# Windowed attention and a rational feed-forward: unpadded float32 scores in row halves, and an order of issue left to the scheduler

## The chip, the core and the metric

The kernel runs on one core of a Trainium2 chip. The metric is device microseconds from start to end of one execution; a run's time is set beside the median of several. The engines are named as the profile names them: PE (TensorE, matrix products and transposes), PEld (its weight loads), DVE (VectorE), ACT (ScalarE), POOL (GpSimd) and SP (SyncE, which here only issues transfers). Each engine takes its instructions in one order, fixed when the program is built.

## The reference

Two parts in a row: attention with a window and a few global keys, and a feed-forward network whose activation is a ratio of polynomials.

```python
scores = q @ k.T / 8 - 2.0 ** -(h + 1) * dist        # per head h; B, H, S, D = 4, 8, 768, 64
keep = (key < n_global) | ((0 <= rel) & (rel < n_local))   # n_global = 8, n_local = 96
a = softmax(where(keep, scores, -1e9))
x = concat_heads(a @ v)                              # 3072 tokens x 512
h = x @ w_in                                         # 512 x 2048
g = (a0 + a1*h + a2*h**2 + a3*h**3) / (1 + |b0|*|h| + |b1|*h**2 + 1e-6)
out = g @ w_out                                      # 2048 x 512
```

All inputs are float32 but for the weights' and coefficients' stored form, which the kernel decodes. With a window of 96 a block of 128 queries needs its own block of keys and the one before it; the eight global keys are copied over columns of the older block that are no longer needed.

## The kernel before

The work is cut into 96 attention units: a unit is one block of 128 tokens and one pair of heads (2 x 64 columns), four units to a block, eight to a chunk of 256 tokens. `unit(u)` gives the chunk, the block, the pair p, the batch and the block's number i in its batch. Units 0 to 23 (`PLAIN = 24`), which are the first batch, work in plain float32; the later ones work in a split of two parts, and are not changed. Each unit goes through steps: `st_load` (q and k of two units in one transfer each), `st_qkT` (transposes of q and k on PE), `st_qkE` (they are scaled out of PSUM), `st_score` (products on PE, then masks and row minimum in one DVE operation for each head, `tensor_tensor_reduce`), `st_soft` (exponential on ACT), `st_sums`, `st_norm` (POOL), `st_pT` (transposes of the probabilities), `st_pv` (product with v) and `st_x`. The feed-forward of a chunk runs in steps `st_ffn1`, `st_ew1` to `st_ew4` and `st_ffn2` some ten units behind; in the first chunk its products are plain float32 too. Weights come as 32 transfers of 512 KB that SP issues (`fetch`), and are decoded on ACT, POOL and DVE (`decode`) and later split (`split_w`).

In the early units a head's keys fill 64 of the 128 rows of the array, as two heads share a transposed tile. The kernel multiplies all 128 rows: `qz` holds for each head a copy of q in which the other head's 64 rows are zero (cleared once at the start, three buffers in turn), and `kF` the keys of the current and the previous block:

```python
nc.scalar.activation(out=qz[ds_, x, :], in_=tk[ds_, 0, :], func=AF.Copy, scale=float(2.0 ** (2 * p + x - 2)))
nc.scalar.copy(out=pl.kF[:, p, i % 2, :], in_=tk[:, 1, :])
nc.tensor.matmul(out=blocks_of(s_ps[:, x], i), lhsT=qT[:, x, :], rhs=blocks_of(pl.kF[:, p], i), ...)
```

Transposes, scores and products with v take turns in three PSUM banks (`ps_t`, `bufs=3`); a score tile `s` holds both heads of a unit in one bank. The product with v of two heads writes to different halves of the array's columns (`o_ps[x * D:(x + 1) * D]`).

Order: the loop over t gives each step a priority (`PRI_A` in the first part, `PRI` behind), and a scheduler that estimates times lists each engine's instructions by it. On top of that `ORDER` is a written list for PE, DVE, ACT, POOL and SP that fixes the order of the first steps, up to about unit 36 and the feed-forward step 25, some 320 us; `pin()` chains the instructions in that order and puts all others behind. Behind it the scheduler's order holds.

Of the kernel before, what the change touches and what calls it, by code (L numbers as in the profile page):

```python
# [9 lines left out]
F32 = mybir.dt.float32  # L10
FR = mybir.dt.float32r
# [35 lines left out]


ORDER = dict(
    PE=(  # L50
# [25 lines left out]
    ),  # L76
    DVE=(
# [132 lines left out]
def tile_kernel(ctx: ExitStack, tc: tile.TileContext, q, k, v, n_global, n_local,  # L210
# [258 lines left out]
    sp = {}  # L469
    tqk = {}  # L470
    qTs = {}
    prob = {}
    pTs = {}
    ops = {}

# [500 lines left out]
```

## Time and profile before

| | |
|---|---|
| median of 3 runs | 748.33 us (747.7 to 750.04) |
| profiled execution: span from first to last instruction | 747.0 us |
| PE busy | 723.6 us (97%) |
| DVE, ACT, POOL busy | 605.0, 576.5, 457.2 us |
| granted clock of PE, mean | 0.996 |

The profiled execution's own time is its span; the runs' times include what lies around it. Busy time is an average over parts of the kernel with different limits, so the rows below are taken by stretch. An idle time in brackets or behind an arrow names what ended it. Matmuls are pipelined, and their ends are modelled: the time from one start to the next is a better price of a matmul in a run than its duration.

### The profile page before, as it was taken

To read this page: it belongs to the slowest core of one execution; us is meant where nothing else is said; L and a number is where in the kernel's file an instruction comes from. 1 tells how busy PE (TensorE), PEld (TensorE's weight loads), DVE (VectorE), ACT (ScalarE), POOL (GpSimd) and SP (SyncE) were. 2 spreads that over 40 slices of the span, in tenths; PEclk is the share of its full clock that TensorE was granted. 3 is DMA by queue.
4 is the path that set the end of the run, shared out by engine and by line. 5 is a ranking of instruction groups with operands and counts; after the bars stand their busy time and mean duration, and the time that the engine had idled before them with its cause. 6 is when DMAs were issued, how large, how long until landed. Compare 5 with 4: busy or idle time off the path is not lost.

```text
span 747.0 us, 15315 instructions
## 1 busy us (share of the span) xinstructions
PE 723.6 (97%) x5026; PEld 629.0 (84%) x5026; DVE 605.0 (81%) x1437; ACT 576.5 (77%) x1303; POOL 457.2 (61%) x504
## 2 busy tenths in 40 slices
PE   5799899999999999999999999999999999999996
PEld 4576566888988989999999999998998989998995
DVE  5888978888889797878888888887888888875565
ACT  6889776887987886877887878877877878866664
POOL 3366997776576675655665657656666566664441
PEclk9999999999999999999999999999999999999999
DMA  8986310124535443334334334334434333210000
GB/s 252 300 271 195 99 30 15 50 58 103 140 106 139 141 115 90 115 108 109 110 96 119 114 104 123 115 101 99 125 92 125 117 87 98 84 48 2 29 1 33
DMA packets 123581, 79.49 MB, mean 106 GB/s; under 512 B 82532, under 2 KB 104036, under 8 KB 123492
## 3 DMA queue, kind: packets, MB, share of 16 engines
q1 hardware_dynamic: 122288, 77.89, 36.4%
q8 instruction: 42, 0.69, 0.4%
q10 hardware_dynamic: 1204, 0.52, 0.3%
q14 instruction: 47, 0.39, 0.2%
HBM read 35.92 MB, written 6.29 MB: 57 GB/s over the span
## 4 chain that ended last, share of the span: by engine, by line
PE 86%; DVE 4%; DMA 4%; ACT 3%; issue 2%; POOL 1%; SPq 0%; DVEq 0%; ACTq 0%; POOLq 0%
PE h L374 34%; PE acc L450 32%; PE o L623 5%; PE s L541 5%; PE tp L597 3%; DMA r<-in_moe_w_in_dram 2%; PE acc L445 2%; PE s L536 2%; PE tk L486 1%; PE h L366 1%; DMA vt<-in_v_dram 1%; ACT pr L565 1%; DMA nat<-in_q_dram 1%; DVE w_3f L310 0%; DVE pr L555 0%
## 5 line engine op out<-in xcount | busy, mean ns | idle before, releaser
L581 POOL TENSOR_SCALAR pr<-pr,stats 128x256 f32<-128x256 f32 (+1 forms) x176 | 157.6, 906 | 75.5 <-DVE stats L572 46.7
L374 PE MATMUL h<-xh,win_l 128*128 128x256 f32 x704 | 198.2, 282 | 0.0
L407 POOL TENSOR_TENSOR fa<-fa,fs 128x512 f32<-128x512 f32 x95 | 123.7, 1302 | 100.4 <-ACT fs L400 88.8
L450 PE MATMUL acc<-wout_l,g 128*128 128x512 f32 x352 | 139.3, 396 | 0.0
L374 PEld LDWEIGHTS h<-xh,win_l 128*128 128x128 f32 x704 | 133.1, 189 | 2.3 <-issue 1.4
L430 POOL TENSOR_TENSOR g<-fu,g 128x512 fp32r<-128x512 f32 x87 | 113.9, 1309 | 34.4 <-ACT g L429 23.1
L398 ACT ACTIVATE fu<-h,coef 128x512 f32<-128x512 f32 (+1 forms) x97 | 74.9, 772 | 41.0 <-PE h L374 37.5
L565 ACT ACTIVATE pr<-pr,stats 128x256 f32<-128x256 f32 (+1 forms) x192 | 92.9, 487 | 16.9 <-DVE stats L555 16.4
L419 DVE SCALAR_TENSOR_TENSOR fu<-fu,coef,q 128x512 f32<-128x512 f32 (+1 forms) x97 | 71.6, 738 | 24.7 <-ACT q L415 23.3
L414 ACT ACTIVATE fs<-fa,coef 128x512 f32<-128x512 f32 (+1 forms) x97 | 69.6, 717 | 27.1 <-POOL fa L407 25.5
L405 DVE TENSOR_TENSOR fu<-fu,h 128x512 f32<-128x512 f32 (+1 forms) x97 | 65.8, 678 | 29.8 <-ACT fs L400 27.4
L450 PEld LDWEIGHTS acc<-wout_l,g 128*128 128x128 f32 x352 | 66.2, 188 | 11.9
L518 ACT ACTIVATE kq<-tk 64x256 fp32r<-64x256 f32 x144 | 54.3, 377 | 26.9 <-DVE kq L519 15.8
L406 DVE SCALAR_TENSOR_TENSOR fu<-fu,coef,h 128x512 f32<-128x512 f32 (+1 forms) x97 | 71.7, 739 | 2.0
L420 DVE SCALAR_TENSOR_TENSOR q<-fa,coef,q 128x512 f32<-128x512 f32 (+1 forms) x97 | 72.2, 744 | 0.0
L600 DVE COPY pT<-tp 128x512 f32<-128x512 f32 (+1 forms) x75 | 48.4, 646 | 25.1 <-PE tp L597 24.4
L400 ACT ACTIVATE fs<-h,coef 128x512 f32<-128x512 f32 (+1 forms) x97 | 66.2, 682 | 2.6 <-DVE fu L421 1.1
L519 DVE SCALAR_TENSOR_TENSOR kq<-tk,kq 64x256 fp32r<-64x256 f32 x144 | 60.8, 422 | 8.6 <-ACT kq L518 4.2
L421 DVE SCALAR_TENSOR_TENSOR fu<-q,fu 128x512 f32<-128x512 f32 (+1 forms) x97 | 66.1, 682 | 1.6
L399 ACT ACTIVATE fa<-h,coef 128x512 f32<-128x512 f32 (+1 forms) x97 | 65.5, 676 | 0.3 <-DMA out_dram<-o 0.3
L429 ACT CAST g<-fu 128x512 fp32r<-128x512 f32 (+1 forms) x89 | 54.9, 617 | 8.4 <-DVE fu L421 7.5
L415 ACT ACTIVATE q<-fs 128x512 f32<-128x512 f32 (+1 forms) x97 | 57.2, 590 | 0.9
(258 smaller groups left out, 2008.4 us busy)
## 6 DMA issues: line engine op xcount, KB each, us to landing
pm<-pr SPq DMA_DIRECT2D x60, 256.0 KB
mv<-nat SPq DMA_DIRECT2D x36, 256.0 KB
qT<-kq SPq DMA_DIRECT2D x144, 64.0 KB
r<-in_moe_w_in_dram SPq DMA_DIRECT2D x16, 512.0 KB
r<-in_moe_w_out_dram SPq DMA_DIRECT2D x16, 512.0 KB
nat<-in_q_dram SPq DMA_DIRECT2D x48, 128.0 KB
vt<-in_v_dram SPq DMA_DIRECT2D x48, 128.0 KB
nat<-in_k_dram SPq DMA_DIRECT2D x46, 128.0 KB
```

Source lines behind the costliest of these rows:

```text
L374: nc.tensor.matmul(out=hps[f][:, y, :], lhsT=w[:, fs], rhs=x[:, ct, :], start=(n == 0), stop=(n == 3 * NCT - 1))
L398: nc.scalar.activation(out=u, in_=h, func=AF.Identity, scale=a3, bias=a2)
L400: nc.scalar.activation(out=s, in_=h, func=AF.Square, scale=b1)
L406: nc.vector.scalar_tensor_tensor(out=u, in0=u, scalar=a1, in1=h, op0=ALU.add, op1=ALU.mult)
L407: side(f).tensor_tensor(out=a, in0=a, in1=s, op=ALU.add)
L414: nc.scalar.activation(out=s, in_=a, func=AF.Ln, bias=q1)
L419: nc.vector.scalar_tensor_tensor(out=u, in0=u, scalar=a0, in1=r, op0=ALU.add, op1=ALU.mult)
L420: nc.vector.scalar_tensor_tensor(out=r, in0=a, scalar=q1, in1=r, op0=ALU.add, op1=ALU.mult)
L430: side(f).tensor_tensor(out=g[:, 1, ys], in0=u, in1=g[:, 0, ys], op=ALU.subtract)
L450: nc.tensor.matmul(out=acc, lhsT=gs[f][:, z, y, ts], rhs=w, start=(ft == 0 and n == 0), stop=(ft == NFT - 1 and n == 2))
L565: nc.scalar.activation(out=d, in_=d, func=AF.Exp, scale=-1.0, bias=st[:, x:x + 1], accum_out=st[:, 2 + 2 * x:3 + 2 * x])
L581: nc.gpsimd.tensor_scalar(out=d, in0=d, scalar1=st[:, 6 + x:7 + x], scalar2=None, op0=ALU.mult)
```

## The change

For units 0 to 23 the padded `qz` falls away. `kF` gets a third slot for q, and one scaling takes q and k of a unit out of PSUM together, both by 2^(p-1). `st_qkT` transposes two units into one bank, at even t. The new `st_pair` issues the scores of two units: for each unit both heads in turn, head x with rows x*64 to x*64+63 and a bank of its own, chained so that this order holds. The reductions then use a mask at half size for the second head, as in the later units; the half masks are made at the start and not at unit 24. The copy of the global columns (`kGF`) is made on POOL out of `kF`, and copied back for two units at once. `st_pT` of two units is issued at even t. `ORDER`, `pin` and `traced` are removed, so the scheduler orders everything.

```diff
-ORDER = dict(
-    PE=("qkT0 score0:1 qkT1 score0:1 score1 qkT2:1 pT0:1 qkT2:1 pT0:1 score2 qkT3 pT1 pv0:6 score3:1 ..."),
...
     def st_qkT(u):
+        kind, unit_r = (FR, ident_r) if u >= PLAIN else (F32, ident)
+        tk = pl.ps_t.tile([P, 2, 2, P], kind, tag="t", name=f"tk{u}")
+        for y in range(2):
+            for z in range(2):
+                n = nat[u // 2][:, 1 - z, 2 * y:2 * y + 2, :]
+                nc.tensor.transpose(out=tk[:, y, z, :], in_=n.rearrange("p a d -> p (a d)"), identity=unit_r)
+            tqk[u + y] = tk[:, y]
...
         if u < PLAIN:
-            qz = pl.qz[:, u % 3]
-            for x in range(2):
-                ds_ = slice(x * D, (x + 1) * D)
-                nc.scalar.activation(out=qz[ds_, x, :], in_=tk[ds_, 0, :], func=AF.Copy,
-                                     scale=float(2.0 ** (2 * p + x - 2)))
-            nc.scalar.copy(out=pl.kF[:, p, i % 2, :], in_=tk[:, 1, :])
+            nc.scalar.activation(out=pl.kF[:, p, i % 2:3:2 - i % 2, :], in_=tk, func=AF.Copy, scale=half)
             if i == 0:
-                nc.scalar.copy(out=pl.kGF[:, p, :], in_=tk[:, 1, 0:G])
-            qTs[u] = qz
+                nc.gpsimd.tensor_copy(out=pl.kGF[:, p, :], in_=pl.kF[:, p, 0, 0:G])
             return
...
+    def st_pair(u):
+        c, t, p, b, i = unit(u)
+        banks = [pl.ps_t.tile([P, 2, 2, P], F32, tag="t", name=f"s{u + x}") for x in range(2)]
+        began = len(nc.cur_bb.bb.instructions)
+        for y in range(2):
+            for x in range(2):
+                own = pl.kF[x * D:(x + 1) * D, p + y]
+                nc.tensor.matmul(out=blocks_of(banks[x][:, y], i), lhsT=own[:, 2, :], rhs=blocks_of(own[:, 0:2, :], i),
+                                 start=True, stop=True)
+            sps[u + y] = [banks[x][:, y] for x in range(2)]
+        run = list(nc.cur_bb.bb.instructions)[began:]
+        for x, y in zip(run, run[1:]):
+            behind_of(y, x, "row halves in turn")
+        if 1 <= i < NT - 1:
+            nc.gpsimd.tensor_copy(out=pl.kF[:, p:p + 2, i % 2, 0:G], in_=pl.kGF[:, p:p + 2, :])
...
-            m0, m = (mask0, masks) if u < PLAIN or x == 0 else (pl.half0, pl.halves)
+            m0, m = (half0, halves) if x else (mask0, masks)
...
-                scale=-(2.0 ** -(h + 1 if u < PLAIN else 2 * p + 1)), scalar=3e38, op0=ALU.add, op1=ALU.min, accum_out=st[:, x:x + 1])
+                scale=-(2.0 ** -(2 * p + 1)), scalar=3e38, op0=ALU.add, op1=ALU.min, accum_out=st[:, x:x + 1])
...
-        pl.kF = pl.early.tile([P, NPAIR, 2, P], F32, name="kF")
+        pl.kF = pl.early.tile([P, NPAIR, 3, P], F32, name="kF")
...
-        for x in range(2):
-            nc.gpsimd.memset(pl.qz[(1 - x) * D:(2 - x) * D, :, x, :], 0.0)
...
+        for m, full_m in ((half0, mask0), (halves, masks)):
+            nc.vector.tensor_scalar(out=m, in0=full_m, scalar1=0.5, scalar2=None, op0=ALU.mult)
...
+            if t % 2 and t < PLAIN:
+                on("score", st_pair, t - 1)
...
-            if t - 2 < PLAIN:
+            if t % 2 == 0 and t - 2 < PLAIN:
                 on("pT", st_pT, t - 2)
+                on("pT", st_pT, t - 1)
...
-        pin()
```

## Rows read from the trace of the kernel before

**Rows 1.** Busy microseconds (and instructions) of each engine by stretch, granted clock, DMA.
```profile
core 0: us, PE busy (x) PEld busy (x) DVE busy (x) ACT busy (x) POOL busy (x), PEclk, DMA share, GB/s
0.00:36.00 36.00, 23.73 (x128) 16.23 (x128) 25.34 (x100) 25.22 (x87) 11.39 (x33) 0.95 0.92 276
36.00:80.00 44.00, 41.71 (x220) 30.37 (x221) 38.41 (x90) 37.41 (x92) 30.49 (x38) 1.00 0.72 230
80.00:115.00 35.00, 33.53 (x156) 22.16 (x154) 30.18 (x58) 25.78 (x59) 32.04 (x30) 1.00 0.15 38
115.00:165.00 50.00, 49.84 (x316) 39.95 (x317) 42.71 (x94) 40.08 (x94) 36.19 (x33) 1.00 0.14 36
165.00:320.00 155.00, 154.41 (x1156) 139.79 (x1156) 132.50 (x330) 124.15 (x285) 101.91 (x113) 1.00 0.43 120
320.00:680.00 360.00, 360.00 (x2672) 327.42 (x2671) 297.71 (x710) 283.24 (x622) 220.82 (x240) 1.00 0.36 102
680.00:747.00 67.00, 60.36 (x386) 53.06 (x385) 38.16 (x61) 40.64 (x70) 24.32 (x19) 0.98 0.05 18
```
**Rows 2.** The chain that ended last, 0 to 62 us: start, length, what.
```profile
5.63 7.70 DMA r<-in_moe_w_in_dram
...
22.91 0.18 ACT qz L505
...
31.87 0.04 ACT kF L507
```
**Rows 3.** The same chain, 62 to 125 us.
```profile
70.72 2.84 DVE w_3f L310 x2
...
113.09 1.68 DVE w_14f L310
```
**Rows 4.** Busy time by stretch, of the early units' score line (L536) alone.
```profile
0.00:36.00 36.00, 10.61 (x32) 6.90 (x32) 0.95 0.92 276
36.00:115.00 79.00, 10.76 (x40) 6.95 (x40) 1.00 0.47 145
115.00:165.00 50.00, 6.73 (x24) 4.21 (x24) 1.00 0.14 36
```
**Rows 5.** PE in order of time, 150 to 166 us: start, length, line, operation.
```profile
155.15 1.02 PE L536 MATMUL s<-kF,qz 128*128 128x256 f32 x4
156.01 0.38 PE L492 MATMUL tk<-ident,nat 128*128 128x128 f32 x2
```
**Rows 6.** PE in order of time, 60 to 80 us.
```profile
66.52 0.66 PE L623 MATMUL o<-pT,vt 128*64 128x128 f32 x8
67.11 1.13 PE L536 MATMUL s<-kF,qz 128*128 128x256 f32 x4
```
**Rows 7.** PE in order of time, 286 to 296 us.
```profile
288.94 1.97 PE L623 MATMUL o<-pT,vt 128*64 128x128 f32 x32
290.84 0.50 PE L450 MATMUL acc<-w_10h,g 128*128 128x512 f32 x1
```
**Rows 8.** Groups of ACT's instructions by line and shape, 0 to 180 us.
```profile
line engine op names shapes xcount | busy us, mean ns | idle before us <-releasers
L505 ACT ACTIVATE qz<-tk 64x128 f32<-64x128 f32 x48 | 12.9, 268 | 7.8 <-PE tk L492 7.5
...
L507 ACT COPY kF<-tk 128x128 f32<-128x128 f32 x24 | 6.4, 265 | 0.3
...
L600 ACT COPY pT<-tp 128x256 f32<-128x256 f32 x4 | 1.5, 372 | 0.0
```
**Rows 9.** The same view of DVE, 0 to 180 us.
```profile
L555 DVE CUSTOM_DVE_ANT_0 pr<-s,masks 128x256 f32<-128x256 f32 x40 | 15.4, 418 | 2.4 <-PE s L536 1.5 <-PE tp L597 0.7
```
**Rows 10.** Who waited for whom, 0 to 130 us: total us, times, longest.
```profile
ACT w_13f L305 <- DMA r<-in_moe_w_out_dram: 2.8, 1, 2.8
...
PE s L536 <- DVE stats L555: 1.6, 1, 1.6
```
**Rows 11.** The waits of SP's own queue, 0 to 130 us.
```profile
SPq L627 <- PE o L623: 25.8, 5, 14.8
SPq L244 <- PE tk L492: 19.9, 4, 11.4
```

More of the change, by code (lines that the diff above doesn't have):

```diff
@@ L46 @@
 LO_V = (13, 15, 17, 19, 21, 23, 25, 27, 29, 31)
-ORDER = dict(
-    PE=(
[25 rows of a table removed]
-    ),
-    DVE=(
[25 rows of a table removed]
-    ),
-    Activation=(
[19 rows of a table removed]
-    ),
-    Pool=(
[11 rows of a table removed]
-    ),
-    SP=(
[9 rows of a table removed]
-    ),
-)
 PRI = dict(load=0, score=50, soft=100, sums=120, ffn1a=150, qkT=200, pv=250, qkE=300, x=350, split=400, ew3=450, norm=500,
@@ L468, in tile_kernel @@
     masks = const.tile([P, 3, P], BF16, name="masks")
+    half0 = const.tile([P, P], BF16, name="half0")
+    halves = const.tile([P, 3, P], BF16, name="halves")
     sp = {}
@@ L471, in tile_kernel @@
     qTs = {}
+    sps = {}
     prob = {}
@@ L479, in st_qkT @@
     def st_qkT(u):
-        p = unit(u)[2]
-        if u >= PLAIN:
-            tk = pl.ps_t.tile([P, 2, 2, P], FR, tag="t", name=f"tk{u}")
-            for y in range(2):
-                for z in range(2):
-                    n = nat[u // 2][:, 1 - z, 2 * y:2 * y + 2, :]
-                    nc.tensor.transpose(out=tk[:, y, z, :], in_=n.rearrange("p a d -> p (a d)"), identity=ident_r)
-                tqk[u + y] = tk[:, y]
-            return
-        tk = pl.ps_t.tile([P, 2, P], F32, tag="t", name=f"tk{u}")
-        for z in range(2):
-            n = nat[u // 2][:, z, 2 * (p % 2):2 * (p % 2) + 2, :]
-            nc.tensor.transpose(out=tk[:, z, :], in_=n.rearrange("p a d -> p (a d)"), identity=ident)
-        tqk[u] = tk
+        kind, unit_r = (FR, ident_r) if u >= PLAIN else (F32, ident)
[5 more added lines that the diff above has]
+            tqk[u + y] = tk[:, y]
     def st_qkE(u):
@@ L513, in st_qkE @@
         raw = tk.bitcast(F32)
-        half = float(2.0 ** (p - 1))
         for x in range(2):
@@ L527, in st_qkE, with behind_of @@
         qTs[u] = qT
+    def behind_of(x, prev, why):
+        tc.add_manual_dep(x, prev.name, mybir.DependencyInfo(mybir.DependencyClass.NoSync,
+                                                             mybir.DependencyReason.DATA), reason=why)
+    def st_pair(u):
[13 more added lines that the diff above has]
+            nc.gpsimd.tensor_copy(out=pl.kF[:, p:p + 2, i % 2, 0:G], in_=pl.kGF[:, p:p + 2, :])
@@ L529, in st_score @@
     def st_score(u):
         c, t, p, b, i = unit(u)
-        qT = qTs.pop(u)
-        s_ps = pl.ps_t.tile([P, 2, 2, P], F32, tag="t", name=f"s{u}")
-        for x in range(2):
-            h = 2 * p + x
-            if u < PLAIN:
-                nc.tensor.matmul(out=blocks_of(s_ps[:, x], i), lhsT=qT[:, x, :], rhs=blocks_of(pl.kF[:, p], i),
-                                 start=True, stop=True)
-                continue
-            rhs = pl.kq[:, h, 0:2, :] if i else pl.kq[:, h, 0:1, :].broadcast_to([P, 2, P])
-            for z, lhsT in enumerate((pl.kq[:, h, 2, :], qT[:, x, :])):
-                nc.tensor.matmul(out=s_ps[:, x], lhsT=lhsT, rhs=rhs, start=(z == 0), stop=(z == 1))
@@ L542, in st_score @@
-        if 1 <= i < NT - 1 and u < PLAIN:
-            nc.gpsimd.tensor_copy(out=pl.kF[:, p, i % 2, 0:G], in_=pl.kGF[:, p, :])
-        elif 1 <= i < NT - 1:
+        if u < PLAIN:
+            s_ps = sps.pop(u)
+        else:
+            qT = qTs.pop(u)
+            s_ps = pl.ps_t.tile([P, 2, 2, P], F32, tag="t", name=f"s{u}")
+            for x in range(2):
+                h = 2 * p + x
+                rhs = pl.kq[:, h, 0:2, :] if i else pl.kq[:, h, 0:1, :].broadcast_to([P, 2, P])
+                for z, lhsT in enumerate((pl.kq[:, h, 2, :], qT[:, x, :])):
+                    nc.tensor.matmul(out=s_ps[:, x], lhsT=lhsT, rhs=rhs, start=(z == 0), stop=(z == 1))
+            s_ps = [s_ps[:, x] for x in range(2)]
@@ L545, in st_score @@
+        if 1 <= i < NT - 1 and u >= PLAIN:
             hs = slice(2 * p, 2 * p + 2)
@@ L555, in st_score @@
             nc.vector.tensor_tensor_reduce(
-                out=blocks_of(pr[:, x], i), in0=blocks_of(s_ps[:, x], i), in1=mask(x),
-                scale=-(2.0 ** -(h + 1 if u < PLAIN else 2 * p + 1)), scalar=3e38, op0=ALU.add, op1=ALU.min, accum_out=st[:, x:x + 1])
+                out=blocks_of(pr[:, x], i), in0=blocks_of(s_ps[x], i), in1=mask(x),
+                scale=-(2.0 ** -(2 * p + 1)), scalar=3e38, op0=ALU.add, op1=ALU.min, accum_out=st[:, x:x + 1])
         prob[u] = (pr, st)
@@ L662, in windowed @@
         pl.early = scope.enter_context(tc.tile_pool(name="early", bufs=1))
-        pl.kF = pl.early.tile([P, NPAIR, 2, P], F32, name="kF")
+        pl.kF = pl.early.tile([P, NPAIR, 3, P], F32, name="kF")
         pl.kGF = pl.early.tile([P, NPAIR, G], F32, name="kGF")
-        pl.qz = pl.early.tile([P, 3, 2, P], F32, name="qz")
         nc.scalar.dma_start(out=ni[:, 0:2], in_=n_local.bitcast(I32).partition_broadcast(1))
@@ L675, in windowed @@
         make_identity(nc, ident)
-        for x in range(2):
-            nc.gpsimd.memset(pl.qz[(1 - x) * D:(2 - x) * D, :, x, :], 0.0)
         nc.vector.tensor_copy(out=ident_r, in_=ident)
@@ L689, in windowed @@
         window_masks(nc, scr, mask0, masks, nl, ng)
+        for m, full_m in ((half0, mask0), (halves, masks)):
+            nc.vector.tensor_scalar(out=m, in0=full_m, scalar1=0.5, scalar2=None, op0=ALU.mult)
         load_coef()
         base = tc.cur_priority
-        here = nc.cur_bb.bb
-        made, began = {}, len(here.instructions)
-        def traced(token, fn, *args):
-            n = len(here.instructions)
-            fn(*args)
-            for x in list(here.instructions)[n:]:
-                made.setdefault((token, x.engine), []).append(x)
-        def behind_of(x, prev, why):
-            tc.add_manual_dep(x, prev.name, mybir.DependencyInfo(mybir.DependencyClass.NoSync,
-                                                                 mybir.DependencyReason.DATA), reason=why)
-        def halve_masks():
-            for m, full_m in ((pl.halves, masks), (pl.half0, mask0)):
-                nc.vector.tensor_scalar(out=m, in0=full_m, scalar1=0.5, scalar2=None, op0=ALU.mult)
-        def pin():
-            for name, words in ORDER.items():
-                eng = getattr(mybir.EngineType, name)
-                chain, taken = [], {}
-                for word in words.split():
-                    token, _, count = word.partition(":")
-                    own = made[token, eng]
-                    a = taken.get(token, 0)
-                    b = taken[token] = a + int(count) if count else len(own)
-                    chain += own[a:b]
-                for x, y in zip(chain, chain[1:]):
-                    behind_of(y, x, "order of the first steps")
-                known = {x.name for x in chain}
-                for x in list(here.instructions)[began:]:
-                    if x.engine == eng and x.name not in known and "Boundary" not in type(x).__name__:
-                        behind_of(x, chain[-1], "behind the first steps")
         def turn(f):
@@ L750, in behind @@
             def behind(n):
-                now, past = t - n, t - n - 1
-                return [u for u in ((past,) if past >= PLAIN else ()) + ((now,) if now < PLAIN else ())]
+                past = t - n - 1
+                return [past] if past >= PLAIN else [t - 1, t] if t % 2 and t < PLAIN else []
             if t % 2 == 0:
@@ L768, in windowed @@
                 pl.kG = pl.late.tile([P, H, G], FR, name="kG")
-                pl.halves = pl.late.tile([P, 3, P], BF16, name="halves")
-                pl.half0 = pl.late.tile([P, P], BF16, name="half0")
-                tc.cur_priority = base + 1000 * t
-                traced("halves", halve_masks)
                 on("split", st_move, t)
             ffn("ffn1a", st_ffn1, f, 0)
-            if t < PLAIN or t % 2 == 0:
+            if t % 2 == 0:
                 on("qkT", st_qkT, t)
@@ L811, in windowed @@
                 for key in pieces(kind, j):
-                    traced("dec" + "".join(map(str, key)), decode, key)
+                    decode(key)
             if step:
```

9 lines of the change are left out of this document (4 added, 5 removed), and 89 rows, old and new, of tables (Activation, DVE, PE, Pool).

## Prediction

> **What bounds the kernel now.** I read the busy time by stages first, since an average over 747 us hides that the kernel has three parts [rows 1]. From 165 to 680 us TensorE (PE) is busy 154.4 of 155 and 360.0 of 360 us at full granted clock: nothing but PE work counts there. From 0 to 36 us it idles 12.3 us of 36, and the 16 DMA engines are busy 92% of the time. From 36 to 115 us PE idles only 3.8 us, but VectorE (DVE) is busy 68.6 of 79 us and GpSimd (POOL) 32.0 of 35 us in the second half: several engines are close to full. From 115 us on PE is full. All the idle time of PE is 747.0 - 723.6 = 23.4 us: 12.3 before 36 us, 3.8 up to 115, 0.8 up to 320, and 6.6 behind 680 us. The change touches only units 0 to 23, whose scores are done by 165 us, so it can save PE work and can move the first two of these idle sums; the last part it only shifts.
>
> Then the chain that ended last, to see which stage lets a saving through. Up to 62 us it runs over weight transfers (one piece of 7.7 us) with short stretches of ScalarE (ACT) between, nine of them copies of q and k, from 22.91 to 31.87 us, 2.0 us together [rows 2]. Up to 115 us it goes over the decoding of weights on DVE, 2.84 us for two operations at 70.7 us, 1.68 at 113 [rows 3]. Only behind that is it PE nearly without a break. So a microsecond of PE work is worth a microsecond after 115 us, something between nothing and that from 36 to 115, and nothing before 36.
>
> **The change part by part.** *Scores in row halves.* A float32 product is two PE instructions. Four of them, both heads of a unit, take 0.86 us from start to next start (155.15 to 156.01) [rows 5]: 0.215 us for 256 columns, and by columns 0.108 for 128. Two units in a run are 8 x 0.215 = 1.72 us today. With 64 rows for each head the two heads sit in different halves of the array's rows; if they run side by side, the second head's first instruction starts with the first head's second, and eight instructions take five places: 5 x 0.215 = 1.08. No row of before shows row halves. The nearest are the two heads of the product with v, which sit in different halves of the columns, in the same order: eight instructions of 128 columns take 0.59 us to the next start [rows 6], against 8 x 0.108 = 0.86 one by one and 0.54 for five places; 32 take 1.90 us [rows 7], against 3.44 and, for 17 places, 1.83. So such halves do run side by side, at a price of 0.05 to 0.07 us a run. I take 1.72 - 1.08 - 0.05, about 0.6 us, saved for a pair of units. The score instructions lie 32 before 36 us, 40 from 36 to 115 and 24 behind [rows 4], four to a unit: 8, 10 and 6 units, so 4, 5 and 3 pairs. Behind 115 us the 3 pairs save 1.8 us in full; the 5 pairs before it up to 3.0, of which I take half, 1.5, because DVE and POOL are nearly as full as PE there; those before 36 us nothing. Together -3.3; ends -1.8 and -4.8, and 0 if the halves don't overlap.
>
> The Trainium skill (TensorEngine Tiling (Array Packing), Key Properties) speaks against this: changing the tiling mode drains TensorE, and this change goes into the row mode and out of it twelve times. The trace agrees only in that a run with column halves costs 0.05 to 0.07 us over its places [rows 6, 7]; by the rule alone, with a price left open, the sum would lie somewhere above mine. Its other condition (Gotcha 1), that row halves don't share a PSUM bank, the new code meets: each head has a bank of its own.
>
> *One copy of q and k.* Today a unit costs ACT two scalings of 64x128 and a copy of 128x128: 2 x 0.268 + 0.265 = 0.80 us [rows 8]. The new form is one scaling of 128x256; the nearest row of that size out of PSUM takes 0.372 [rows 8]. That is 0.43 us a unit and 10 us of ACT over 24 units, but ACT limits only where the chain crosses it: 2.0 us in the nine pieces [rows 2], of which the same share, 54%, is 1.1. Weight transfers stand next in line there, so I take -0.5; ends 0 and -1.1. The copy of the eight global columns of four units goes from ACT to POOL and each copy back into the keys serves two units; the two clears of the padding fall away; the two halvings of the masks go to the start. POOL is busy 11.4 us of the first 36 and DVE 25.3 [rows 1], so I cost these at nothing; without that cover they would be fractions of a microsecond.
>
> *Two units at a time.* Of the three banks that transposes, scores and products with v share, one pair now holds two until four reductions over them have run. One takes 0.418 us [rows 9], so 1.7 us at the least, and more when a decode of 1 to 2 us stands between [rows 3]. Behind a score that waits for a bank stand, in PE's order, the feed-forward matmuls. Before, one such wait of 1.6 us is in the trace for 24 units [rows 10]. One in each of the 8 pairs behind 36 us would be 12.8, none 0. A pair holds twice as much half as often, so I stay near the one row and add +0.4. The even unit's scores wait for the odd one's copy, about 0.4 us, hidden in the transfers of the fill and later behind feed-forward work. Both transposes of a load now run together, so its buffer comes free one unit earlier; SP waited 19.9 us for such transposes in the first 130 us [rows 11]. The loads would start sooner, in a stage where DMA is 92% busy [rows 1], so they compete with the weights: 0.
>
> *The order of issue.* The written order of PE, DVE, ACT, POOL and SP falls away for roughly the first 320 us. What it is worth, the trace shows only by its neighbour: from 320 to 680 us, where the scheduler already orders, PE idles 0.0 us of 360 [rows 1]. Wherever PE has a backlog, another order costs nothing. Before 115 us it can cost: engines take their queues in order, and an instruction placed too early stops all behind it, as ACT did for 2.8 us on a late weight [rows 10], and SP for 14.8 us behind a single wait at the line that rereads the global rows of v [rows 11]; behind such a wait on SP stand the fetches of weights, for which decode, then feed-forward, wait. At best all idle time of PE from 36 to 115 us goes, -3.8; at worst one more hold of SP reaches PE, +14.8. The order before already contains waits of both kinds and still leaves PE 3.8 us of idle time, so another list is likelier to add than to remove. I take +0.6, about a third of one wait of the 1.6 us kind.
>
> **The sum.** -3.3 - 0.5 + 0.4 + 0.6 = -2.8 us. The profiled execution spans 747.0 us and the median of the runs is 748.3, so 1.3 us lie around the span or between runs. The span would be 744.2, the median 745.5. For this kernel 0.3% is 2.2 us, about the least that can be told from no change: same means 746.1 to 750.6.
>
> **The rivals.** *The new order costs more than the scores save (slower).* Place: the fill and the decoding, before 115 us. Mechanism: SP or ACT held by a wait placed too early, so that weights come later and the feed-forward starts later. For it: the waits of rows 10 and 11, and a stage in which DMA, DVE and POOL are all nearly full. Against it: PE's backlog from 115 us. It decides from 5 us of new idle time on (2.8 + 2.2); one hold of 5 to 15 us gives 748 + 2 to 748 + 12, so 751 to 760. Chance 0.31.
>
> *The saving is hidden.* What bounds 36 to 115 us is decoding on DVE and POOL, so only the 1.8 us behind 115 us stay, and a wait for a bank or a slightly worse order takes them: 746 to 750. For it: the chain over DVE up to 115 us [rows 3]. Chance 0.20.
>
> *The row halves do not run side by side, or each change of mode drains the array.* Then the heads run one behind the other, with the ACT gain alone: 748 - 0.5 + 1.0, about 749. If each of the 24 changes of mode cost as much as an instruction of 256 columns, 0.215, that would be 5.2 us in all and 2.6 for the 12 behind 115 us and the others with weight one half, against 3.3 saved. For it: no row shows row halves. Against it: rows 6 and 7. Chance 0.06.
>
> *The fill gets shorter.* ACT freed by 10 us and loads that start sooner pull the feed-forward forward by 2 to 4 us on top of the scores: 739 to 742. For it: the nine pieces on ACT [rows 2]. Against it: the transfers on the same chain. Chance 0.07.
>
> **How the numbers follow.** The forecast (scores overlap, the order costs 0 to 1.5 us) has a chance of 0.36 and its own range is 742 to 746. Faster by over 0.3%: 0.36 + 0.07 = 0.43. Same: 0.20 + 0.06 = 0.26. Slower: 0.31. The range from 739 to 758 takes in the short fill and most of the slow case, and leaves out the ends of it, about 0.1, and what lies below 739, under 0.05. Nothing holds the order's price closer than its two ends do.
>
> **What would show it.** Right: eight score instructions that start within 1.1 us, PE's busy time down by some 6 us over all 12 pairs, one scaling of about 0.37 us a unit on ACT, PE idle before 115 us still near 16 us, and no idle time from 115 to 680. Wrong in the scores: starts 0.215 apart, or a gap ahead of each run. Wrong in the order: PE idle before 115 us well over 16 us, with ACT or SP waiting for a transfer, or weight fetches issued later. Wrong in the banks: score instructions that wait for reductions pair after pair. The forecast falls if the start of the full stage moves by more than 3 us in either direction, for whatever reason.

## The result, and the profile after

The changed kernel takes 755.52 us (median; 754.89 to 756.21), beside 748.88 for the kernel before in the same comparison: a ratio of 1.0083, with a 95% interval of 1.0066 to 1.0100. It is slower by some 6 us, where I had forecast 3 us faster. The profiled execution spans 754.0 us. The stretches that answer to [rows 1]:

```profile
core 0: us, PE busy (x) PEld busy (x) DVE busy (x) ACT busy (x) POOL busy (x), PEclk, DMA share, GB/s
0.00:36.00 36.00, 23.55 (x146) 16.61 (x148) 27.71 (x108) 24.08 (x72) 11.59 (x34) 0.95 1.01 300
36.00:80.00 44.00, 36.92 (x194) 26.13 (x192) 40.97 (x84) 35.14 (x78) 31.56 (x35) 0.92 0.71 228
80.00:115.00 35.00, 32.63 (x125) 20.85 (x126) 24.47 (x51) 19.25 (x38) 25.38 (x23) 0.90 0.05 12
115.00:165.00 50.00, 50.00 (x338) 39.96 (x336) 34.96 (x84) 38.09 (x83) 34.60 (x33) 1.00 0.14 35
165.00:320.00 155.00, 152.79 (x1113) 136.00 (x1110) 132.44 (x330) 124.76 (x284) 100.26 (x113) 1.00 0.42 116
320.00:680.00 360.00, 360.00 (x2690) 327.41 (x2689) 297.16 (x715) 283.99 (x626) 222.40 (x242) 1.00 0.37 103
680.00:754.00 74.00, 67.33 (x430) 59.10 (x429) 43.08 (x69) 44.85 (x77) 26.85 (x21) 0.97 0.05 16
```

From 36 to 115 us PE idles 9.4 us (7.1 and 2.4), against 3.8 before, and its granted clock is 0.92 and 0.90 where it was 1.00. All its idle time up to 115 us is 21.9 us, against 16.0. The fill (up to 36 us) and the full stage from 115 to 165 us are as they were; 165 to 320 us has 1.6 us more idle time. So most of the loss, 5.7 us, is idle time from 36 to 115 us, in whose first part DVE is busy 41.0 of 44 us. And PE's busy time, 723.2 us against 723.6, has hardly fallen, where I had named some 6 us.

PE in order of time there:

```profile
64.01 1.97 PE L529 MATMUL o<-pT,vt 128*64 128x128 f32 x16 [1.15 <-ACT pT L506]
67.70 2.08 PE L342 MATMUL acc<-w_2f,fu 128*128 128x512 f32 x2 [1.71 <-DVE fu L318]
...
73.13 3.62 PE L263 MATMUL h<-x,w_2f 128*128 128x256 f32 x16
82.37 6.35 PE L263 MATMUL h<-x,w_2f 128*128 128x256 f32 x16 [5.62 <-DVE fu L303]
...
92.00 0.82 PE L503 MATMUL tp<-ident,pr 128*128 128x128 f32 x6
92.75 0.70 PE L428 MATMUL s<-kF 64*128 64x256 f32 x2
```

Two holds, 1.71 and 5.62 us, both for the feed-forward's elementwise work on DVE (`st_ew4` at L318, `st_ew2` at L303); they are 7.3 of the 9.4 us that PE idles from 36 to 115 us, and no wait of PE in that time ends with a sum or a norm. Near them the same work takes longer: ahead of the first, 16 products with v take 1.97 us and not 1.09 as in a run shown further down (k1); behind the second, 16 feed-forward products take 6.35 and not 3.62. The clock, by stretches of 4 us:

```profile
64.00:68.00 4.00, 2.27 (x17) 0.50 0.57 197
...
84.00:88.00 4.00, 4.00 (x12) 0.53 0.00 0
```

0.50 of 2.4 GHz is the lower level, 1.2 GHz; each time PE had been idle for part of the microseconds ahead of it. Idle time alone doesn't decide it: k1 has the same work and as much idle time just ahead of 64 us, and its clock stays at 1.00. Nor do the times follow the clock: the four runs of the changed kernel, with mean clocks of 0.986 to 0.994, lie within 1.3 us, and the one with the highest clock takes 755.28 us. Behind the scores that start at 61.73 us there are none until 92.75, 31 us later; before, the longest such time up to 115 us was 12 us. DVE in the same time:

```profile
63.11 1.06 DVE L207 SCALAR_TENSOR_TENSOR w_3f<-w_3f,r 128x512 int32<-128x512 int32 x1
64.09 1.76 DVE L209 SCALAR_TENSOR_TENSOR w_3f<-r,w_3f 128x512 int32<-128x512 int32 x1
65.77 0.67 DVE L302 TENSOR_TENSOR fu<-fu,h 128x512 f32<-128x512 f32 x1
66.36 0.68 DVE L207 SCALAR_TENSOR_TENSOR w_3f<-w_3f,r 128x512 int32<-128x512 int32 x1
66.97 0.68 DVE L318 SCALAR_TENSOR_TENSOR fu<-q,fu 128x512 f32<-128x512 f32 x1
...
77.08 1.15 DVE L207 SCALAR_TENSOR_TENSOR w_13f<-w_13f,r 128x512 int32<-128x512 int32 x1
...
79.47 0.14 DVE L476 TENSOR_REDUCE stats<-stats 128x2 f32<-128x4 f32 x1
...
81.58 0.74 DVE L303 SCALAR_TENSOR_TENSOR fu<-fu,coef,h 128x512 f32<-128x512 f32 x1
...
83.78 0.15 DVE L478 RECIPROCAL stats<-stats 128x2 f32<-128x2 f32 x1
```

Decoding of weights (L207, L209) fills the queue ahead of what PE waits for: 6.0 of the 9.8 us from 69.72 to 79.47. The step that ends the hold of 5.62 us is L303 at 81.58. The sums of unit 12 come at 79.47 and its reciprocal at 83.78, though its exponentials ended at 69.98: 14.0 us from their end to the end of the reciprocal, 13.2 for unit 13, against 2.2 and 3.8 before. The norms on POOL need the reciprocals and start at 84.59, the transposes of the probabilities need the norms, and the next scores stand behind those transposes in PE's order. So the late sums hold back no product of PE directly; they take away the scores that could have stood in the holds.

The scores themselves. A whole run, a run cut in two, and the scaling on ACT:

```profile
164.17 1.14 PE L428 MATMUL s<-kF 64*128 64x256 f32 x8
165.23 0.44 PE L503 MATMUL tp<-ident,pr 128*128 128x128 f32 x2
```
```profile
127.72 0.70 PE L428 MATMUL s<-kF 64*128 64x256 f32 x2
128.35 0.39 PE L271 MATMUL h<-xh,w_0h 128*128 128x256 f32 x1
...
132.55 1.13 PE L428 MATMUL s<-kF 64*128 64x256 f32 x6
133.61 0.39 PE L271 MATMUL h<-xh,w_1h 128*128 128x256 f32 x1
```
```profile
L396 ACT ACTIVATE kF<-tk 128x256 f32<-128x256 f32 x24 | 7.8, 377 | 7.8 <-PE tk L385 7.8
```

The row halves do run side by side: eight instructions take 1.06 us to the next start against 1.72 [rows 5]. In the trace they start as four pairs, 7 ns apart within a pair and 0.215 us from pair to pair, except that the first step is 0.320. So a run is four places and not the five of my model, and, as I read the longer first step and the end, about 0.105 us each on going in and coming out (4 x 0.215 + 2 x 0.105 = 1.07). But seven of the twelve runs are cut: the order puts other work between them, as I read it because the second head's bank is not free yet. Two instructions alone take 0.63 and the other six 1.06, together 1.69. A cut run saves nothing. By adding up the times from start to next start, without idle time, the early scores take 19.3 us against 23.3 before.

### The profile page after: what moved, and what is told of

It is laid out like the page before. It is cut to its first block, busy times and chain, and to the rows that moved or that the text cites. A ratio compares the mean times of both kernels' runs of the same rounds, so it can differ in the third digit from the quotient of the medians.

```text
span 754.0 us, 15278 instructions
## 1 busy us (share of the span) xinstructions
PE 723.2 (96%) x5026; PEld 626.1 (83%) x5026; DVE 600.8 (80%) x1435; ACT 570.2 (76%) x1253; POOL 452.6 (60%) x498
## 4 chain that ended last, share of the span: by engine, by line
PE 85%; DVE 6%; ACT 3%; DMA 2%; issue 2%; POOL 1%; SPq 1%; POOLq 0%; ACTq 0%; DVEq 0%
PE h L271 32%; PE acc L347 31%; PE o L529 5%; PE s L448 4%; PE h L263 3%; PE tp L503 3%; PE acc L342 3%; PE tk L385 2%; PE s L428 2%; DMA r<-in_moe_w_in_dram 1%; ACT pr L471 1%; DVE pr L461 1%; ACT m L202 1%; DVE m L207 1%; DVE fu L316 0%
## 5 line engine op out<-in xcount | busy, mean ns | idle before, releaser
L487 POOL TENSOR_SCALAR pr<-pr,stats 128x256 f32<-128x256 f32 (+1 forms) x176 | 155.3, 895 | 93.1 <-DVE stats L478 47.8
L302 DVE TENSOR_TENSOR fu<-fu,h 128x512 f32<-128x512 f32 (+1 forms) x97 | 65.7, 677 | 40.5 <-ACT fs L297 40.2
L303 DVE SCALAR_TENSOR_TENSOR fu<-fu,coef,h 128x512 f32<-128x512 f32 (+1 forms) x97 | 71.7, 739 | 2.0
L405 ACT ACTIVATE kq<-tk 64x256 fp32r<-64x256 f32 x144 | 54.3, 377 | 24.6 <-DVE kq L406 12.1
L406 DVE SCALAR_TENSOR_TENSOR kq<-tk,kq 64x256 fp32r<-64x256 f32 x144 | 60.7, 422 | 9.2 <-ACT kq L405 5.1
L318 DVE SCALAR_TENSOR_TENSOR fu<-q,fu 128x512 f32<-128x512 f32 (+1 forms) x97 | 66.2, 682 | 1.7
L326 ACT CAST g<-fu 128x512 fp32r<-128x512 f32 (+1 forms) x89 | 54.9, 616 | 14.0 <-DVE fu L318 13.3
```

Source lines behind the costliest of these rows:

```text
L303: nc.vector.scalar_tensor_tensor(out=u, in0=u, scalar=a1, in1=h, op0=ALU.add, op1=ALU.mult)
L487: nc.gpsimd.tensor_scalar(out=d, in0=d, scalar1=st[:, 6 + x:7 + x], scalar2=None, op0=ALU.mult)
```

## Experiments

Ratios are to the kernel before, run beside each. They come from different comparisons, in which that kernel's median was 748.4 to 749.3.

### The order alone, and a written order

The kernel before with its list no longer applied, so that the scheduler orders it all:

```diff
-        pin()
```


> The kernel before, with the written order taken away and nothing else: the scheduler orders everything. Theory A (the lost microseconds are the price of the order, in the filling and decoding stage before 115 us): 3 to 9 us slower than before, 752 to 757, with PE idle before 115 us at 19 to 25 us instead of 16. Rival B (they come from handling two units at a time, which holds banks and delays the even unit, whatever the order): within 2 us of before, 746 to 750.5.

Measured: 750.03 us, 1.0014 (1.0004 to 1.0024). The loss of the list costs the old kernel about 1 us; my term was 0.6. So the order is not the loss by itself. Then the changed kernel under a list merged from the old one, with the steps of a pair at the odd unit's place, and the same with the run's products ordered by head:

```diff
+        pin()
```
```diff
-        for y in range(2):
-            for x in range(2):
+        for x in range(2):
+            for y in range(2):
```


> The changed kernel under the written order of before, with only those steps moved that two units at a time force (both scores of a pair in one run behind the transposes of the unit before, both reductions and exponentials together, the product with v behind the run). Theory A: faster than before by the saved PE work behind 36 us, 3 to 5 us, so 743 to 746, with eight score instructions in about 1.06 us to the next start. Rival B: still slower than before, 750 or more, with PE waiting for banks or for the even unit before 115 us.

> As e2, but a run goes through one head's rows first (both units) and then the other head's, so the halves meet only once: seven places of 0.215 us instead of five. If the halves run side by side only when neighbours differ: a run takes about 1.5 us to the next start, and the kernel is 2 to 4 us slower than e2. Rival (a drain at each change, or no overlap at all): the run takes as long as in e2, and the times agree within 1 us.

Measured: 782.47, 1.0457 (1.0435 to 1.0478), and 781.94, 1.0449 (1.0428 to 1.0469). The merged list is a poor one (PE waits 8.0 us for norms on POOL and 7.9 for copies on ACT), so it tells nothing of what a good one would give. It does show that the order within a run is indifferent: either way the starts come in four pairs, and a run takes 1.06 or 1.07 us.

### Row halves and two units at a time, each alone

```diff
 # g1_one_unit: the changed kernel, one unit a step
-        for y in range(2):
+        for y in (0,):
...
-            if t % 2 and t < PLAIN:
-                on("score", st_pair, t - 1)
+            if t - 1 < PLAIN:
+                on("score", st_pair, t - 1)
```


> The changed kernel's unpadded scores in the row halves (one copy of q and k, one scaling, two banks), but one unit at a time: two transposes, two products side by side, and reductions, exponentials, norms and transposes of probabilities in the step in which the kernel before has them; the scheduler orders issue. Theory T (the two-at-a-time staging is the loss, not the row halves): PE's idle time before 115 us goes back from 21.9 to about 16 to 17 us and the time to 747 to 750 (ratio 0.998 to 1.002). Theory H (the halves themselves, each run with 0.105 us on entering and on leaving and two of three banks held): time stays 753 to 757, idle time over 20 us. A unit's two 256-column products take two places of 0.215 us and twice 0.105, about 0.64 us, against 0.86 padded.


```diff
 # g2_padded_two: the kernel before without pin(), two units a step
+        for u in (u0, u0 + 1):
+            qT = qTs.pop(u)
...
+            for x in range(2):
+                nc.tensor.matmul(out=blocks_of(sps[u][:, x], i), lhsT=qT[:, x, :],
+                                 rhs=blocks_of(pl.kF[:, unit(u)[2]], i), start=True, stop=True)
...
+            if t % 2 and t < PLAIN:
+                on("score", st_pair, t - 1)
```


> The kernel before without its written order (750.03 us), with the padded q and full-height scores kept, but staged two units at a time as the changed kernel does it: four transposes into one bank, four products, two units' reductions, exponentials, norms and transposes of probabilities in one step of two. Theory T (the staging is the loss): 755 to 759 us, ratio 1.008 to 1.014, with the idle stretch of PE around 65 to 85 us as in the changed kernel. Theory H (the row halves are): 749 to 751, ratio 1.000 to 1.003.

Measured: g1 768.96, 1.0261 (1.0235 to 1.0287); g2 758.63, 1.0126 (1.0102 to 1.0151). Theory H falls with g2 and theory T with g1, which is slower than either had it: the two parts don't add up. Two units at a time cost the padded kernel 1.1%, 8 us, against e1; given that, the row halves win 0.4%, 3 us, nearly the 3.8 us that I had put on them and on ACT. One unit at a time in halves is the worst of these four. Its PE:

```profile
64.19 0.70 PE L429 MATMUL s<-kF 64*128 64x256 f32 x2
64.82 1.12 PE L342 MATMUL acc<-w_0f,fu 128*128 128x512 f32 x2
...
66.73 0.70 PE L429 MATMUL s<-kF 64*128 64x256 f32 x2
67.36 0.44 PE L386 MATMUL tk<-ident,nat 128*128 128x128 f32 x2
```

The two heads of a unit run 2.5 us apart, at 0.63 us each: 1.26 where the padded unit takes 0.86. Nine of its 24 units are cut so, and its early scores take 24.1 us from start to next start, more than the 23.2 of e1.

### What in the staging: cadence, probability buffers, banks

```diff
 # f1_cadence: what follows the products one unit a step
-            if t % 2 == 0 and t - 2 < PLAIN:
+            if t - 2 < PLAIN:
                 on("pT", st_pT, t - 2)
-                on("pT", st_pT, t - 1)
```


> The changed kernel with its products still two units at a time, but reductions, exponentials, sums, norms and transposes of probabilities put back to one unit per step. If the clustering of the work behind the scores on DVE, ACT and POOL is the loss, the time falls to 749 to 752 us (ratio 1.001 to 1.004) and the 5.6 us idle stretch at 76.8 us shrinks below 3; if it is the pairing of the products themselves (two banks held by a run of two units), it stays at 754 to 757.


```diff
 # g3_prob4
-        pr = pl.att.tile([P, 2, 2, P], F32, tag="prob", name=f"pr{u}")
+        pool = pl.early if u < PLAIN and u // 2 % 2 == 0 else pl.att
+        pr = pool.tile([P, 2, 2, P], F32, tag="prob", name=f"pr{u}", bufs=2)
```


> The changed kernel with four buffers for probabilities of early units in place of two, nothing else. Two units at a time fill both of two buffers, so the next two units' reductions wait for the transposes of the last two. Theory P (that ring is the loss): 748 to 752 us, ratio 0.999 to 1.004, and idle time before 115 us falls from 21.9 to about 17. Otherwise unchanged, 754 to 757.

Measured: f1 759.8, 1.0150 (1.0127 to 1.0172), no better but worse, outside both ranges; g3 754.49, 1.0071 (1.0051 to 1.0090), its interval over that of the changed kernel. Neither is the cause. Next the banks: one taken away from the padded kernel, and a fourth for the early units (the transposes of q and k in a bank of their own, the reciprocal `q` in SBUF).

```diff
 # h1_two_banks: the kernel before without pin()
+        idle = pl.ps_t.tile([P, 2, 2, P], F32, tag="t", name="idle")
+        nc.vector.memset(idle[:, 0, 0, 0:1], 0.0)
...
+            if t == PLAIN - 1:
+                nc.vector.tensor_copy(out=stats[:, 0, 0:1], in_=idle[:, 0, 0, 0:1])
```


> The kernel before without its written order (750.03 us), with one of the three PSUM banks that transposes, scores and attention products share taken away up to unit 22: padded scores of one unit a time, nothing else. Theory K (the loss of the changed kernel is that its scores hold two of the three banks at once, and nothing of what surrounds them can proceed): 757 to 770 us, ratio 1.011 to 1.028, PE idle before 115 us above 20 us. Rival (the banks are not what binds; the clustered work behind two units is): 749 to 753, ratio 1.000 to 1.005.


```diff
 # h2_after_bank4, h3_one_bank4, h4_before_bank4
+        tk = (pl.ps_t if u >= PLAIN else pl.ps_x).tile(...)
-            rps[f] = pl.ps_r.tile(sh, F32, tag="r", name=f"q{f}")
+            rps[f] = (pl.ps_r if pl.ps_r else pl.early).tile(sh, F32, tag="r", name=f"q{f}", bufs=1)
```


> The changed kernel with a fourth bank for the early units: the q and k transposes get a bank of their own, and the reciprocal of the feed-forward, which had it, lies in SBUF up to unit 23. Theory K: 747 to 751 us (ratio 0.997 to 1.003), idle before 115 us below 18 us. Rival: 753 to 757.

> One unit at a time in the row halves (768.96 us with three banks), with the fourth bank in the same way. Theory K: most of the 19 us return, 748 to 755 us (ratio 0.998 to 1.008). Rival: 763 to 770.

> The control: the kernel before without its written order, with the fourth bank in the same way. It tells what the bank and the move of the reciprocal into SBUF are worth by themselves. Theory K: little, 747 to 751 us (ratio 0.997 to 1.002), since one unit's padded scores hold one bank of three already. If it gains as much as the changed kernel gains by it, banks are short everywhere and say nothing of the change.

Measured: h1 769.59, 1.0272 (1.0232 to 1.0311); h2 774.04, 1.0312; h3 768.68, 1.0257; h4 766.05, 1.0218 (1.0194 to 1.0241). A bank less costs the padded kernel 19 us, so banks can matter that much. But the control with the fourth bank lost 16 us by itself (PE there waits 9.2 us for the single bank of the transposes, `tk<-ACT kF`), so h2 and h3 are inconclusive on the changed kernel. Only h3 loses nothing by the same move (g1 had 768.96); that banks are short in g1 would explain it, if the move costs as much there, which no run shows.

### Sums ahead of decoding

The trace of the changed kernel showed the sums of units 12 and 13 stuck behind decodings. The edge: from the step of unit 12 on, a decoding's DVE instructions stand behind the reciprocals emitted ahead of them. It is a place in DVE's queue and no wait. It was put into the changed kernel, into the padded one staged by twos, and, last, as a control into the old kernel.

```diff
 # k1_sums_first (k3: the same in g2; k5: in e1; k6: in g1)
                 for key in pieces(kind, j):
+                    began = len(nc.cur_bb.bb.instructions)
                     decode(key)
+                    for x in list(nc.cur_bb.bb.instructions)[began:]:
+                        if x.engine == mybir.EngineType.DVE and t >= 12:
+                            behind_of(x, last_sum[-1], "sums ahead of decoding")
```


> The changed kernel, with DVE's decoding of the last weights (from the step of unit 12 on) put behind the sums and reciprocals of the two units ahead of them; nothing else. In the changed kernel these sums wait 7.4 us and the reciprocals 4.3 us more behind decodings, and PE has no attention work between 62 and 93 us. Theory C (two units at a time bunch the attention work, and what follows a bunch is late on a DVE that has no idle time): the next scores start near 82 in place of 92.7 us, PE's hold of 5.6 us at 76.8 shrinks, and the time falls by 3 to 6 us, to 749 to 752. Theory K alone (two of three banks held): the time stays 754 to 757.

> The same edge in the kernel with padded scores two units at a time (758.63 us). Theory C: 3 to 6 us fall away, 752 to 756, since its sums stand behind the same decodings. Theory K alone: 757 to 760.

> The control: the kernel before without its written order (750.03 us), with the edge that brought the changed kernel from 755.5 to 742.3 us (decodings on DVE behind the sums, from the step of unit 12 on). Theory C (the late sums are a loss of the bunched staging): this kernel has attention work in PE every 5 to 14 us already, so that it moves by 2 us at most, 748 to 751 (ratio 0.999 to 1.003). Rival (the edge mends a fault of the scheduler's order that every version has, and the row halves have no part in the 742): 741 to 745.

> One unit at a time in the row halves (768.96 us) with the same edge. Theory C with K (one at a time in the halves loses by its banks, two of three held for each unit): the edge gives back at most 5 us, 762 to 768 (ratio 1.018 to 1.026). If late sums are its loss too: 745 to 755.

| ratio to the kernel before | padded, without the edge | with it | row halves, without | with it |
|---|---|---|---|---|
| one unit at a time | e1 1.0014 | k5 1.0029 | g1 1.0261 | k6 1.0149 |
| two units at a time | g2 1.0126 | k3 1.0075 | the change 1.0083 | **k1 0.9923** |

The changed kernel with the edge takes 742.28 us, 0.9923 (0.9901 to 0.9945): 12 to 13 us faster than the changed kernel (by the ratios, by the medians) and 6 faster than the one before, faster than any other version run here. I had expected 3 to 6. The control goes to 750.96 (1.0018 to 1.0040) and gains nothing, though its sums still come some 6 and 4 us behind the exponentials (units 12 and 13), so that it got the edge's effect only in part. k3 gains 4 us (755.01, 1.0053 to 1.0098), k6 9 us (759.88, 1.0132 to 1.0166), more than the 5 that I had allowed it and too little for the other theory.

So the late sums cost where the row halves or the pairing is there, and not only where units are paired: the edge is worth 9 us to the halves alone, 4 to the pairing alone, 12 to 13 to both and nothing to neither. In g1 and g2 the reciprocals of units 12 and 13 come 9 to 11 us behind the exponentials, and PE stands still for the norm that waits for the first of them (g1, then g2; its reciprocal ends at 85.7 and 88.2 us):

```profile
88.15 0.69 PE L504 MATMUL tp<-ident,pr 128*128 128x128 f32 x2 [7.71 <-POOL pr L488]
89.59 0.69 PE L600 MATMUL tp<-ident,pr 128*128 128x128 f32 x2 [5.63 <-POOL pr L584]
```

In k6 and k3 no wait for a norm is left from 36 to 115 us. PE of k1, whose scores up to 61.7 us start within 0.3 us of those of the changed kernel:

```profile
64.18 1.09 PE L531 MATMUL o<-pT,vt 128*64 128x128 f32 x16 [1.32 <-ACT pT L508]
65.21 1.12 PE L342 MATMUL acc<-w_2f,fu 128*128 128x512 f32 x2
...
69.18 3.62 PE L263 MATMUL h<-x,w_2f 128*128 128x256 f32 x16
...
76.07 2.75 PE L263 MATMUL h<-x,w_2f 128*128 128x256 f32 x12
...
79.41 0.70 PE L429 MATMUL s<-kF 64*128 64x256 f32 x2
```

and its DVE, and POOL's norms behind it:

```profile
63.73 0.68 DVE L302 TENSOR_TENSOR fu<-fu,h 128x512 f32<-128x512 f32 x1
64.33 0.68 DVE L318 SCALAR_TENSOR_TENSOR fu<-q,fu 128x512 f32<-128x512 f32 x1
...
70.44 0.16 DVE L477 TENSOR_REDUCE stats<-stats 128x2 f32<-128x4 f32 x1 [0.47 <-ACT pr L472]
...
72.22 0.16 DVE L479 RECIPROCAL stats<-stats 128x2 f32<-128x2 f32 x1
...
72.34 0.74 DVE L303 SCALAR_TENSOR_TENSOR fu<-fu,coef,h 128x512 f32<-128x512 f32 x1
```
```profile
73.90 5.08 POOL L489 TENSOR_SCALAR pr<-pr,stats 128x256 f32<-128x256 f32 x4
```

The reciprocal of unit 12 comes 11.6 us earlier, the scores of unit 14 13.3 us earlier, and the holds of 1.71 and 5.62 us are gone (one of 1.38 stands at 82.7). The elementwise work comes earlier too, since the decodings stood ahead of it as well: L302 and L318 by 2 to 2.6 us, and L303, which had ended the hold of 5.62 us, by 9.2 (81.58 to 72.34). The edge moves decoding behind both, and which of the two is worth how much I have not separated; since PE's holds ended with the elementwise work, the name of the edge says less than it does. It also makes the scheduler list all that follows anew, and another edit that should have cost nothing moved the time by 4 us (k2 below), so that not each of the 13 us need come from these holds. The stretches of k1:

```profile
36.00:80.00 44.00, 41.71 (x222) 29.62 (x220) 39.24 (x88) 35.18 (x78) 34.30 (x38) 1.00 0.66 212
80.00:115.00 35.00, 32.51 (x155) 20.46 (x155) 28.43 (x63) 22.03 (x48) 25.26 (x23) 1.00 0.13 34
115.00:165.00 50.00, 49.86 (x343) 41.14 (x343) 36.74 (x88) 40.40 (x88) 40.11 (x38) 1.00 0.21 56
165.00:320.00 155.00, 155.00 (x1160) 140.83 (x1159) 135.11 (x335) 126.65 (x290) 101.36 (x113) 1.00 0.44 119
```

The clock is 1.00 in all of them. Spans and PE's busy time (754.0 and 723.2; 740.2 and 717.9) divide the 13.8 us between the two profiles: 8.4 us less idle time and 5.4 us less busy time. 1.6 us of the idle time lie before 36 us, where k1 has as much more busy time and its scores start at the same times; behind 36 us it is 6.8 and 7.0. 3.7 us of the busy time are float32 feed-forward products (59.9 to 56.1 us from start to next start), which in the changed kernel run at the lower clock level in part.

### The pairing of the transposes, whole runs, and what binds next

```diff
 # k4_padded_tr: the kernel before without pin(), only the transposes by twos
-            if t < PLAIN or t % 2 == 0:
+            if t % 2 == 0:
                 on("qkT", st_qkT, t)
```


> The kernel before without its written order, with only the transposes and the scaling of q and k two units at a time; scores, exponentials, sums, norms and transposes of probabilities stay one unit per step. If the pairing of the products and what follows them is what costs the padded two-unit kernel its 8.4 us, this one is at 749 to 752 (ratio 1.000 to 1.004). If the pairing of the transposes is (loads and a bank wanted for two units at once), 756 to 760.


```diff
 # f2_whole: the changed kernel
+        if u:
+            behind_of(run[0], last_tp[u - 1], "whole run")
```


> The changed kernel with the products of two units held behind the last transpose of the unit ahead of them, so that fewer runs of eight are cut into two and six. A cut run takes 0.62 + 1.06 us, a whole one 1.06, so that nine whole ones give back up to 5 us. If the cut runs are the loss: 750 to 753. If the loss lies in the long stretch without attention work, holding the products back only makes it longer: 755 to 760.

> The changed kernel with the edge, and four buffers for early probabilities in place of two. If the ring of two buffers binds once the sums are in time, 738 to 741 us (ratio 0.986 to 0.990); if not, 742 as with the edge alone.

Measured: k4 761.46, 1.0167 (1.0145 to 1.0189): pairing the transposes alone costs the padded kernel more than the whole staging. I could not trace the 11 us to one wait; the lateness is there too (the reciprocals of units 13 and 14 come 12 and 8 us behind the exponentials), and PE waits 4.1 us for `fu` L406. f2 754.02, 1.0070 (1.0052 to 1.0087), between its two ranges: five runs of twelve still come apart (three by other work between, two by a wait) where the changed kernel cuts seven, so it says little of the cut runs, only that holding the products back gains nothing clear of the intervals. k2 (g3 and the edge together) 746.11, 0.9962 (0.9948 to 0.9976), 4 us behind the edge alone, where I had expected no loss: the ring of two probability buffers is not what binds next, and why more buffers cost time stays open.

## Why the prediction was wrong

**The step that failed** is the pricing of the order of issue (+0.6 us, taken as a third of one 1.6 us wait) and of two units at a time (+0.4, one wait for a bank of that kind) each by itself, and their adding up. The first alone was about right for the old staging: e1 shows 1 us. The second alone was not: g2, the padded kernel staged by twos under the scheduler's order, is 8 us behind e1. And in the changed kernel, where both apply, one edge in the order gives back 12 to 13 us (k1). I read the price of the order from a stretch where PE has a backlog and from a few waits of the old list, as if order were a property of the kernel.

**What was left out.** I priced the banks and not what comes late. Under the scheduler's order the sums of units 12 and 13 are late without the edge, by 9 to 14 us in g1, g2, f1, g3 and the changed kernel, and in e1 too (8.8 and 10.0 us from the exponentials to the reciprocal); the old list had kept them at 2.2 and 3.8. But in e1 scores come every 3 to 15 us from 30 to 115 us, and PE idles 4.4 us from 36 to 115. In the changed kernel both units of a pair wait together, and from 64 to 92 us PE has 16 products with v and four transposes beside the feed-forward, which waits for the same DVE. So the lateness is common to all; what covers it in e1 is missing in the others. That the edge gains 12 to 13 us in the changed kernel and nothing in the old one under the scheduler's order is shown; that the cover is the reason is read from the traces, and it doesn't give the sizes: g1 and k6, with one unit at a time, show that pairing is not the only way to lose it.

**The rival that came nearest** was that the new order costs more, at 751 to 760 us, with 755.5 inside; that its range holds the result is in part luck. The place was right (before 115 us) and the engine wrong: I had SP or ACT held by a wait, and it was DVE, which hardly waits but takes decodings first. Of SP's waits up to 130 us the longest grew to 27.8 us, and no hold of PE from 36 to 115 us ends with a transfer. The rows said so: DVE was busy 38.4 of 44 us [rows 1], and decodings of 2.84 us stood on the chain [rows 3]. I used that to discount the saving, and not as a queue in which something could be late. In the rival on changes of mode a sum is wrong: the three pairs behind 115 us have 6 changes, and with the weights of the scores' own sum it is 11 changes and 2.4 us in all, not 12 and 2.6.

**The scores.** Halves side by side: right. Five places and 0.05 us: wrong in both terms, four and twice 0.105; that the sum is nearly the same (1.07 and 1.13) is luck. A run has 0.21 us over its places. The Trainium skill (TensorEngine Tiling (Array Packing), Key Properties) says that a change of mode drains the array; the trace agrees in that extra time, and no run shows the drain apart. The halved weight up to 115 us hid that runs would be cut, which forfeits the saving of seven. So the scores take 4.0 us less (23.3 to 19.3), and the changed kernel lost that again: its float32 feed-forward products take 59.9 us from start to next start, against 55.1 before. With the edge PE's busy time is 5.7 us below that of before (717.9 against 723.6), near the 6 that I had named, but 4.0 of it are the scores. **ACT**: 377 ns a scaling against 372; right. **Fill**: 12.5 us of idle time against 12.3; no gain, as the sum had it but for 0.5.

**Left open.** Why paired transposes alone cost 11 us (k4). Why the padded kernel by twos stays 5 us behind with the edge (k3): its idle time from 36 to 115 us falls from 12.1 to 5.4, but 3.7 us come back before and behind. With the edge the row halves by twos are 13 us ahead of it, and the scores' own time explains only some 3.5 of them. And what the banks still hold back: in the changed kernel the scores hold two of three banks for 21.3 of the first 115 us, counted from a bank's first score to its last reduction, and practically never before; in k1 it is 26.9, in a faster kernel, so the time held is no price by itself.

## What to carry to other kernels

A reorganisation must be priced by what is left to cover the waits around it, and not only by its own instructions: find the engine that is nearly full there, and ask what urgent instruction (here a sum of 0.14 us, or an elementwise step of 0.7) could stand behind others that are not urgent. A scheduler's order is worth what it is worth for one staging; after a change of staging, look in the trace for the late urgent instruction before judging the change. Here one edge turned a loss of 0.8% into a gain of 0.8%.

## What the runs showed of the hardware

- Instructions in the two row halves start 6 to 14 ns apart in whole runs at full clock, whatever their order in the kernel (e2, e3); a run has about 0.21 us over its places, which I read as 0.105 each on going into the row mode and out of it. Two float32 instructions of 256 columns alone so take 0.63 us, not 0.43 (the changed kernel, g1), and a run pays from one whole unit on (0.63 us in g1 against 0.86 padded).
- A hold of PE can cost more than its length: behind the 5.62 us the granted clock was at its lower level (0.53 from 84 to 88 us) and 16 products took 6.35 us and not 3.62, 2.7 us more; in e1, behind a hold of 3.6 us, it was 0.58 from 72 to 76. It need not fall: before, with PE busy 2.0 of the 4 us from 76 to 80, it stayed at 1.00.
